# Inverse row sums of the attention spread over the partitions by way of DRAM instead of by transpositions, from the fifth pair on

## The chip, the cores and the metric

The kernel runs on one core of a Trainium2 chip. The metric is the device time of one execution in microseconds, as the median of the runs: 739.43 us (739.4 to 740.52, three runs). Engines: TensorE (PE; its weight loads are PEld), VectorE (DVE), ScalarE (ACT), GpSimd (POOL) and SyncE (SP), which here only issues DMAs.

## The reference

It is block-causal attention over 8 batches, 8 heads, 576 positions and a head size of 64, and then a gated MLP whose gate mixes positions. Cut to what matters:

```python
scores = scale * np.matmul(q, k.transpose(0, 1, 3, 2))
scores = np.where(mask, scores, -1000000000.0)
scores = scores - np.max(scores, axis=-1, keepdims=True)
attn = np.exp(scores)
attn = attn / (np.sum(attn, axis=-1, keepdims=True) + 1e-09)
x = np.matmul(attn, v)
h = gelu(x @ w_in); u, v = h[..., :512], h[..., 512:]
v_n = layer_norm(v) * g_ln
v_s = np.einsum('ts,bsd->btd', w_sg, v_n) + b_sg[None, :, None]
return x + (u * v_s) @ w_out
```

The change concerns the division by the row sums.

## The kernel before

**The work.** Attention is done by pairs of heads: 32 pairs, four (Q = 4) to a batch. The 576 rows of a pair are five row tiles (NT = 5), the first of 64 rows and four of 128. `Scores` makes the scores of a row tile on PE (tiles named s); DVE masks them and finds the negative maximum (negm), ACT takes the exponential and adds up each row on the way, into `sums`, a tile of 128 x 5 x 2: partition is the row within its tile, the columns are row tile and head.

**The values.** `Values` turns the exponentials on PE (banks pA, pB, pC for the full blocks, pd for the diagonal ones) and multiplies them with v (bank ob). The result lies transposed: partitions are the 2 x 64 columns of the two heads, the free axis is the 576 rows. So the inverse row sums, which lie one row to a partition, are needed along the free axis and in all 64 partitions of a head. `inverse` (L489) adds 1e-9, takes the reciprocal (r, 128 x 10), and has ACT spread r into rx (128 x 5 x 128, each number 64 times). `turn_sums` (L500) then does ten transpositions on PE, five of the diagonal blocks into pd and five of rx into the rest of pd and into pe, and two ACT copies take both banks to the tile rb. `normalise` (L536) multiplies on DVE with rb into x, and stores x to DRAM (spill). The 64 columns of the first row tile come from a free corner of pe (`self.o0`).

**The order.** One slot of the loop (L977) does pair n: it turns the exponentials of pair n (`turn("A0")` to `"C"`), then `turn_sums`, the first scores of pair n + 1, the products of pair n, `normalise`, the second scores of pair n + 1, and at the end `inverse` and `split_qk` for the pairs ahead. Between these, `hole(k)` places k units of the MLP of the batch before: a v part of 5 units, u, s and o parts of 8 units each, 29 over four slots. In the fourth slot of a batch come the spatial products (s part), in the third the out products (o part, bank acco), which add rows of spill (xr), and so on. In the first four slots (`opening_slot`) and the next four (`middle_slot`, with a list of steps written out by hand, `SCRIPT`) all engines keep the order of the code; these slots also load, split and transform the weights. From the ninth slot on (`slot`) only PE keeps it, and the scheduler orders the other engines' work (L978, L979).

**The queue of SP.** SP issues the DMAs, in each slot: six loads of v (`load_v`), one each of q and k for the pair after next (`load_qk`), the store of x, and loads of xr and stores of the output. In the first slots `fetch` adds weights: its list holds 16 parts of w_in, g_ln (g_bc), five steps of spatial weights (the last with b_sg) and 8 parts of w_out. `middle_slot` of pair 4 begins

```python
if n == Q:
    fetch(5)
load_v(n + 1)
load_qk(n + 2)
```

and its script fetches spatial weights, which POOL splits into ws_h and ws_l before it splits q and k (qh, ql, kh, kl) for pair 6.

Of the kernel before, what the change touches and what calls it, by code (L numbers as in the profile page):

```python
# [9 lines left out]
F32 = mybir.dt.float32  # L10
# [4 lines left out]
ALU = mybir.AluOpType  # L15
# [5 lines left out]
def kernel(  # L21
# [13 lines left out]
    B, H, D, S = qT.shape  # L35
    P = 128
    BLK = 64
# [4 lines left out]
    NT = (S + P - 1) // P  # L42
# [19 lines left out]
    vector = Engine("V", nc.vector)  # L62
# [3 lines left out]
    sync = Engine("S", nc.sync)  # L66

    cp = ctx.enter_context(tc.tile_pool(name="cp", bufs=1))
    sp = ctx.enter_context(tc.tile_pool(name="sp", bufs=1))
    dp = ctx.enter_context(tc.tile_pool(name="dp", bufs=2, space=DRAM))  # L70
# [6 lines left out]
    def page(dtype, n, name):  # L77
        tag, bufs = KINDS.get(name, KINDS["w"])
        return sp.tile([P, n], dtype, tag=tag, name=name, bufs=bufs)

    def bank(name):
        return psum.tile([P, 512], F32, tag="bank", name=name, bufs=8)
# [7 lines left out]
    def turn(out, in_):  # L90
        return tensor.transpose(out, in_, ident)

    def copy(e, dst, src):
        f = {"v": vector.tensor_copy, "a": scalar.copy, "g": gpsimd.tensor_copy}[e]
        return f(dst, src)
# [12 lines left out]
    def load_qk(n):  # L108
        b, h = PAIRS[n]
        q_f = sp.tile([P, S], F32, tag="q_f", name="q_f", bufs=1)  # L110
        k_f = sp.tile([P, S], F32, tag="k_f", name="k_f", bufs=1)
        q = qT[b, h : h + 2].rearrange("a d s -> (a d) s")
        k = kT[b, h : h + 2].rearrange("a d s -> (a d) s")
        if n == 0:
            for c in Q_PARTS:
                sync.dma_start(q_f[:, c], q[:, c])
            for c in K_PARTS:
                scalar.dma_start(k_f[:, c], k[:, c])
        else:
            sync.dma_start(q_f, q)  # L120
            behind["S"] = sync.dma_start(k_f, k)
        raw[n] = (q_f, k_f)

    def split_qk(n):
        out = []
        for x, t in zip(raw.pop(n), "qk"):
            hi = sp.tile([P, S], F32R, tag=t + "h", name=t + "h", bufs=1)
            lo = sp.tile([P, S], F32R, tag=t + "l", name=t + "l", bufs=1)
            if n:
                copy("g", hi, x)  # L130
                behind["G"] = gpsimd.tensor_tensor(lo, x, hi.bitcast(F32), op=ALU.subtract)
            out += [hi, lo]
        qk[n] = out
# [18 lines left out]
    def load_v(n, heads=(0, 1)):  # L152
        b, h = PAIRS[n]
        v_f, v_d = vals[n] = v_bufs[n % 2]
        lo, hi = slice(0, BLK), slice(BLK, P)
        for a in heads:
            r = (lo, hi)[a]
            cols = slice((h + a) * D, (h + a + 1) * D)
            x = v[b, : (NT - 1) * P, cols].rearrange("(j p) d -> p j d", p=P)
            if a == 0:  # L160
                sync.dma_start(v_f[:, :, r], x)
            else:
                sync.dma_start(v_f[lo, :, r], x[hi])
                sync.dma_start(v_f[hi, :, r], x[lo])
            sync.dma_start(v_d[r, : NT - 1, r], x[lo])
            sync.dma_start(v_d[r, NT - 1, r], v[b, S - TAIL :, cols])
# [24 lines left out]
    for s in (0, 1):  # L191
        t = cp.tile([P, NT - 1, 2 * D], F32, name=f"v_f{s}")
        d = cp.tile([P, NT, 2 * D], F32, name=f"v_d{s}")
        for a in (0, 1):
            r = slice(a * D, (a + 1) * D)
# [23 lines left out]
    W = 256  # L219
# [3 lines left out]
    def fetch(k=1):  # L223

        for _ in range(k):
            coming.popleft()()
# [118 lines left out]
    def weight_half():  # L345

        while weights:
            said = next(weights[0][1], None)
            if said is not None:
                return said  # L350
            weights.popleft()
# [106 lines left out]
    Q = H // 2  # L458
# [9 lines left out]
    class Values:  # L468
# [19 lines left out]

        def inverse(self):  # L489

            r = sp.tile([P, NT * 2], F32, tag="ri", name="r", bufs=2)
            vector.tensor_scalar_add(r, self.sm.rearrange("p i a -> p (i a)"), 1e-9)
            vector.reciprocal(r, r)
            self.rx = sp.tile([P, NT, 2 * D], F32, tag="rx", name="rx", bufs=1)
            scalar.copy(
                self.rx.rearrange("p i (a d) -> p (i a) d", a=2),
                r.unsqueeze(2).broadcast_to([P, NT * 2, D]),
            )

        def turn_sums(self):  # L500

            t, t2 = bank("pd"), bank("pe")
            W = NT * BLK
            for i in range(NT):
                c = slice(i * BLK, i * BLK + P)
                first = turned[:, BLK:] if i else ident
                tensor.transpose(t[:, c], pairs[i][:, P * i : P * (i + 1)], first)
            for i in (0, 1):
                turn(t[:, W + i * BLK : W + i * BLK + P], self.rx[:, i, :])
            for i in (2, 3, 4):  # L510
                turn(t2[:, P * (i - 2) : P * (i - 1)], self.rx[:, i, :])
            d = sp.tile([P, W + S], F32, tag="rb", name="rb", bufs=1)
            copy("a", d[:, :512], t)
            copy("a", d[:, 512:], t2[:, : 3 * P])
            self.dg = [d[:, i * BLK : (i + 1) * BLK] for i in range(NT)]
            self.rb = d[:, W:]
            self.o0 = t2[:, 3 * P : 3 * P + BLK]

        def products(self):
# [16 lines left out]
        def normalise(self):  # L536

            x = self.x = page(F32, S, "x")
            vector.tensor_tensor(x[:, BLK:], self.ob, self.rb[:, BLK:], op=ALU.mult)
            vector.tensor_tensor(x[:, :BLK], self.o0, self.rb[:, :BLK], op=ALU.mult)  # L540
            spill[self.b, self.p] = dp.tile([P, S], F32, tag="spill", name="spill", bufs=12)
            sync.dma_start(spill[self.b, self.p], x)

# [21 lines left out]
    def run_gelu():  # L565

        if side and side[0][0] == "G":
            side.popleft()[1]()
# [182 lines left out]
    def hole(k=1):  # L751

        while k > 0 and work:
            try:
                next(work[0])
                k -= 1
            except StopIteration:
                work.popleft()
# [15 lines left out]
    def split_pending():  # L774

        for f in pending:
            f()
        pending.clear()

    def opening_slot(n, va):  # L780

        va.turn("A0")
        va.turn("A1")
        va.turn("B0")
        va.turn("B1")
        va.inverse()
        split_pending()
        va.turn("C")
        load_qk(n + 2)
        load_v(n + 1)  # L790
        fetch(2 if n < Q - 1 else 4)
        nx = Scores(n + 1)
        for p in nx.FIRST:
            nx.products(*p)
        va.turn_sums()
        weight_half()
        for p in nx.FIRST:
            nx.softmax(*p)
        if n < Q - 1:
            nx.second()  # L800
            weight_half()
            split_qk(n + 2)
            weight_half()
            va.products()
            va.normalise()
            pending.append(va.split)
        else:
            weight_half()
            weight_half()
            va.products()  # L810
            va.normalise()
            va.split()
            nx.second()
        nv = Values(n + 1, nx)
        if n == Q - 1:
            nv.inverse()
            split_qk(n + 2)
            weight_half()
        return nx, nv
# [102 lines left out]
    def middle_slot(n, va):  # L922

        script = SCRIPT[n]
        g = [int(x) for x in FIRST[n % Q]]
        if n == Q:
            fetch(5)
        load_v(n + 1)
        load_qk(n + 2)
        va.turn("A0")  # L930
        va.turn("A1")
        if n != 2 * Q - 2:
            split_pending()
        run_gelu()
        hole(g[0])
        script[0]()
        va.turn("B0")
        va.turn("B1")
        hole(g[1])
        script[1]()  # L940
        va.turn("C")
        va.turn_sums()
        hole(g[2])
        script[2]()
        nx = Scores(n + 1)
        nx.first()
        va.products()
        va.normalise()
        nx.second()
        if n % Q == Q - 1:  # L950
            va.split()
        else:
            pending.append(va.split)
        script[3]()
        nv = Values(n + 1, nx)
        nv.inverse()
        split_qk(n + 2)
        script[4]()
        hole(g[3])
        script[5]()  # L960
        return nx, nv
# [70 lines left out]
```

## Time and profile before

| | |
|---|---|
| median of three runs | 739.43 us |
| the profiled execution's own time | 739.77 us |
| its span | 738.0 us |
| granted TensorE clock | 1.00 |
| pairs | 32 |
| DMA packets | 84731, 70.04 MB |

The span runs from the first to the last instruction of the profiled execution. Rows of a timeline or a chain give the start in us, the length in us, the engine, and what was written from what (the program's names) with a count; a bracket tells how long the engine had stood idle before it and what released it. Nearly all instructions are recorded by one helper (L60), so tiles tell them apart, not lines. PE's matmuls overlap: their lengths are longer than their distance, so the chain of waits gives the time that a group of them takes. SPq rows are DMAs issued by SP.

### The profile page before, as it was taken

What the parts mean: (1) busy time and instruction counts of PE and PEld (TensorE: products, weight loads), DVE (VectorE), ACT (ScalarE), POOL (GpSimd) and SP (SyncE); (2) the same over time, 40 slices, a digit from 0 to 9 for tenths busy, and PEclk for the clock granted to TensorE, in tenths of its full rate; (3) what the DMA queues carried; (4) which work ended last, traced back from release to release, by engine and by line L of the source; (5) the groups of instructions that cost most, each with busy time, mean ns of one, the idle gap of its engine ahead of it and who ended that gap; (6) DMA issues with size and microseconds to landing.
All of it is one profiled execution on the core that took longest, in us unless ns stands there. A gap on an engine that the chain in (4) does not pass through costs nothing.

```text
span 738.0 us, 18412 instructions
## 1 busy us (share of the span) xinstructions
PE 730.3 (99%) x6936; PEld 687.4 (93%) x6936; DVE 466.2 (63%) x1461; ACT 431.6 (58%) x1077; POOL 296.0 (40%) x361
## 2 busy tenths in 40 slices
PE   8999999999999999999999999999999999999997
PEld 7888999899998999989999899998999999998997
DVE  6998987579764396544956449554694456841732
ACT  7987888387544874458734577347783376712500
POOL 5767945455451244512345322453233533321120
PEclk9999999999999999999999999999999999999999
DMA  6667333143531225212342122422224221220032
GB/s 166 168 175 232 104 99 112 49 128 120 149 93 40 59 84 181 73 39 67 90 151 73 44 82 71 151 73 66 78 71 133 71 72 42 81 82 0 17 114 96
DMA packets 84731, 70.04 MB, mean 95 GB/s; under 512 B 59938, under 2 KB 60578, under 8 KB 84644
## 3 DMA queue, kind: packets, MB, share of 16 engines
q1 hardware_dynamic: 84356, 68.58, 31.7%
q8 instruction: 55, 0.90, 0.6%
q14 instruction: 32, 0.26, 0.1%
q10 hardware_dynamic: 288, 0.30, 0.1%
HBM read 49.98 MB, written 18.87 MB: 93 GB/s over the span
## 4 chain that ended last, share of the span: by engine, by line
PE 89%; DVE 6%; ACT 2%; issue 1%; DMA 1%; POOL 0%; SPq 0%; ACTq 0%; DVEq 0%
PE accs L60 16%; PE accv L60 14%; PE acco L60 13%; PE accu L60 12%; PE s L60 10%; PE ob L60 10%; PE pA L60 3%; PE pB L60 3%; PE pd L60 3%; ACT prob L60 2%; PE pC L60 2%; PE pe L60 2%; DVE prob L60 2%; DVE vl L60 1%; DMA q_f<-in_qT 0%
## 5 line engine op out<-in xcount | busy, mean ns | idle before, releaser
L60 ACT ACTIVATE prob<-prob,negm 128x576 f32<-128x576 f32 (+3 forms) x320 | 176.5, 554 | 54.7 <-DVE negm L60 53.2
L60 DVE CUSTOM_DVE_ANT_0 prob<-s,mask 128x256 f32<-128x256 f32 (+3 forms) x320 | 119.1, 417 | 40.7 <-PE s L60 39.2
L60 POOL TENSOR_TENSOR xh<-x,xh 128x64 fp32r<-128x64 f32 x32 | 10.8, 336 | 196.5 <-DVE xh L60 166.3
L60 POOL TENSOR_TENSOR gl<-u,gh 128x288 fp32r<-128x288 f32 x64 | 51.9, 814 | 89.0 <-DVE gh L60 73.6
L60 PE MATMUL accu<-xh,wi_h 128*128 128x288 f32 x256 | 78.3, 306 | 0.0
L60 PE MATMUL acco<-gh,wo_h 128*128 128x288 f32 x256 | 77.5, 303 | 0.4 <-DVE negm L60 0.2
L60 PE MATMUL accs<-ws_h,vh 128*128 128x288 f32 x256 | 77.9, 304 | 0.0
L60 PE MATMUL accu<-xl,wi_h 128*128 128x288 f32 x256 | 75.5, 295 | 0.0
L60 PE MATMUL accs<-ws_h,vl 128*128 128x288 f32 x256 | 75.5, 295 | 0.0
L60 PE MATMUL acco<-gh,wo_l 128*128 128x288 f32 x256 | 75.4, 295 | 0.0
L60 PE MATMUL accs<-ws_l,vh 128*128 128x288 f32 x256 | 75.4, 295 | 0.0
L60 PE MATMUL acco<-gl,wo_h 128*128 128x288 f32 x256 | 75.4, 295 | 0.0
L60 PE MATMUL accu<-xh,wi_l 128*128 128x288 f32 x256 | 75.4, 294 | 0.0
L60 DVE TENSOR_TENSOR u<-accs,u 128x288 f32<-128x288 f32 x64 | 29.2, 456 | 58.3 <-PE accs L60 53.6
L60 PE MATMUL accv<-wi_h,xh 128*128 128x512 f32 x160 | 65.3, 408 | 0.0
L60 PE MATMUL s<-kh,qh 64*128 64x320 f32 (+4 forms) x384 | 63.4, 322 | 0.5 <-DVE negm L60 0.5
L60 PE MATMUL accv<-wi_l,xh 128*128 128x512 f32 x160 | 62.8, 393 | 0.0
L60 ACT ACTIVATION_READ_ACCUMULATOR prob<-prob,negm 128x1 f32 x320 | 60.1, 188 | 0.0
L60 PE MATMUL s<-kh,ql 64*128 64x320 f32 (+4 forms) x384 | 59.0, 300 | 0.0
L60 PE MATMUL s<-kl,qh 64*128 64x320 f32 (+4 forms) x384 | 58.0, 299 | 0.0
L60 ACT COPY vv<-accv 128x512 f32<-128x512 f32 x32 | 18.6, 582 | 64.5 <-PE accv L60 64.5
L60 POOL CAST kh<-k_f 128x576 fp32r<-128x576 f32 x31 | 20.7, 667 | 75.7 <-PE s L60 75.7
(119 smaller groups left out, 2093.7 us busy)
## 6 DMA issues: line engine op xcount, KB each, us to landing
spill<-x SPq DMA_DIRECT2D x32, 288.0 KB, 2.7
xr<-spill SPq DMA_DIRECT2D x32, 288.0 KB, 3.1
out_T<-xr SPq DMA_DIRECT2D x32, 288.0 KB, 3.4
q_f<-in_qT SPq DMA_DIRECT2D x31, 288.0 KB, 3.1
k_f<-in_kT SPq DMA_DIRECT2D x31, 288.0 KB, 3.5
v_f<-in_v SPq DMA_DIRECT2D x32, 128.0 KB, 2.8
v_d<-in_v SPq DMA_DIRECT2D x64, 64.0 KB, 2.7
v_f<-in_v SPq DMA_DIRECT2D x64, 64.0 KB, 2.6
```

Source lines behind the costliest of these rows:

```text
L60: return lambda *a, **k: pin(method(*a, **k), self.letter)
```

## The change

For pairs 4 and up `inverse` calls the new `spread`: r is laid out by heads, stored to a DRAM tile of 2 x 640 numbers (a row for each head), and two DMAs read each row back into the 64 partitions of its head, into a part of the tile rb. `turn_sums` for these pairs does only the five transpositions of the diagonal blocks and copies 320 columns; rx, its five transpositions, bank pe and the second copy are not made. `self.o0` moves to a free corner of pd. The five fetches at the start of slot 4 move to the end of slot 3, ahead of the first `spread`.

```diff
         def inverse(self):
 
+            if self.n >= Q:
+                return self.spread()
...
+        def spread(self):
+
+            r = sp.tile([P, 2 * NT], F32, tag="ri", name="r", bufs=2)
+            vector.tensor_scalar_add(
+                r.rearrange("p (a i) -> p a i", a=2), self.sm.rearrange("p i a -> p a i"), 1e-9
+            )
+            vector.reciprocal(r, r)
+            rows = dp.tile([2, NT * P], F32, tag="rows", name="rows", bufs=2)
+            sync.dma_start(rows.rearrange("a (i p) -> p (a i)", p=P), r)
+            self.d = sp.tile([P, NT * (BLK + P)], F32, tag="rb", name="rb", bufs=1)
+            rb = self.d[:, NT * BLK :]
+            for a in (0, 1):
+                sync.dma_start(
+                    rb[a * D : (a + 1) * D, :], rows[a : a + 1, :].broadcast_to([D, NT * P])
+                )
+            self.rb = rb[:, BLK:]
+            self.r0 = rb[:, :BLK]
+
         def turn_sums(self):
 
-            t, t2 = bank("pd"), bank("pe")
+            t = bank("pd")
             W = NT * BLK
             for i in range(NT):
                 c = slice(i * BLK, i * BLK + P)
                 first = turned[:, BLK:] if i else ident
                 tensor.transpose(t[:, c], pairs[i][:, P * i : P * (i + 1)], first)
+            if self.n >= Q:
+                d = self.d
+                copy("a", d[:, :W], t[:, :W])
+                self.dg = [d[:, i * BLK : (i + 1) * BLK] for i in range(NT)]
+                self.o0 = t[:, 512 - BLK :]
+                return
+            t2 = bank("pe")
...
-            vector.tensor_tensor(x[:, :BLK], self.o0, self.rb[:, :BLK], op=ALU.mult)
+            vector.tensor_tensor(x[:, :BLK], self.o0, self.r0, op=ALU.mult)
...
         if n == Q - 1:
+            fetch(5)
             nv.inverse()
...
-        if n == Q:
-            fetch(5)
         load_v(n + 1)
         load_qk(n + 2)
```

More of the change, by code (lines that the diff above doesn't have):

```diff
@@ L511, in turn_sums @@
                 turn(t2[:, P * (i - 2) : P * (i - 1)], self.rx[:, i, :])
-            d = sp.tile([P, W + S], F32, tag="rb", name="rb", bufs=1)
+            d = sp.tile([P, NT * (BLK + P)], F32, tag="rb", name="rb", bufs=1)
             copy("a", d[:, :512], t)
-            copy("a", d[:, 512:], t2[:, : 3 * P])
+            copy("a", d[:, 512 : W + S], t2[:, : 3 * P])
             self.dg = [d[:, i * BLK : (i + 1) * BLK] for i in range(NT)]
-            self.rb = d[:, W:]
+            self.rb = d[:, W : W + S]
+            self.r0 = self.rb[:, :BLK]
             self.o0 = t2[:, 3 * P : 3 * P + BLK]
```

## The prediction

> **What bounds the kernel now.** I read the page first: its busy times and the chain that ended last.
>
> ```profile
> span 738.0 us, 18412 instructions
> PE 730.3 (99%) x6936; PEld 687.4 (93%) x6936; DVE 466.2 (63%) x1461; ACT 431.6 (58%) x1077; POOL 296.0 (40%) x361
> PE 89%; DVE 6%; ACT 2%; issue 1%; DMA 1%; POOL 0%; SPq 0%; ACTq 0%; DVEq 0%
> ```
>
> A busy PE alone proves little, since ends of matmuls are modelled; but the chain agrees: 89% of the time that set the end is PE's, 6% DVE's. Next the busy times by stretches, for four slots and then for one with the out part (columns: stretch, its length, busy us of PE, PEld, DVE, ACT, POOL).
>
> ```profile
> 296.00:390.00 94.00, 94.00 (x922) 89.19 (x922) 56.11 (x188) 53.70 (x135) 33.21 (x40) 1.00 0.29 83
> 346.00:368.00 22.00, 22.00 (x228) 21.52 (x224) 19.50 (x51) 16.52 (x37) 8.06 (x9) 1.00 0.34 98
> ```
>
> PE has no hole in 94 us, at a granted clock of 1.00: work taken from its queue shortens these slots one for one, until another engine stands in the way. DVE is the candidate: 60% over four slots, but 19.5 of 22 us in the slot with the out part. Last the chain of waits inside that slot, around the step that changes (start, length, what):
>
> ```profile
> 361.15 0.44 PE pC L60 x4
> 361.58 0.77 PE pd L60 x7
> 362.35 0.33 PE pe L60 x3
> 362.68 1.60 PE acco L60 x12
> ```
>
> Ten transpositions, seven into pd and three into pe, take 0.77 + 0.33 = 1.10 us, 0.11 each, and PE goes straight on with out products.
>
> **The change, part by part.** *Removed from PE:* five of those ten, 0.55 us per pair, for pairs 4 to 31: 28 x 0.55 = 15.4 us at most. The products still wait for ACT's copy of the diagonal blocks, as now. That copy and the reads write two parts of one tile; it waits for no read if hazards go by region, as they do for wi_l, whose u columns POOL writes while PE reads its v columns:
>
> ```profile
> 60.16 1.29 POOL L60 TENSOR_TENSOR wi_l<-w,wi_h 128x512 fp32r<-128x512 f32 x1
> ```
>
> ```profile
> 60.78 0.39 PE L60 MATMUL accv<-wi_l,xh 128*128 128x512 f32 x1
> ```
>
> *Removed from ACT:* the spreading copy of 0.72 us and the 0.49 us copy of pe; the copy of pd shrinks from 512 to 320 columns.
>
> ```profile
> L60 ACT COPY rx<-r 128x640 f32<-128x640 f32 x32 | 23.1, 723 | 16.6 <-DVE r L60 16.6
> L60 ACT COPY rb<-pe 128x384 f32<-128x384 f32 x32 | 15.6, 486 | 0.0
> ```
>
> That is over 1.2 us of ACT per slot. ACT is 2% of the chain, so I count it at nothing. The freed bank (pe) lets PE run a little further ahead of its readers: also nothing, but only ever a gain. DVE's addition and reciprocal on 128x10 keep their size.
>
> *Added: one DMA that writes 10 x 128 single words to DRAM, and two reads of 2,560 bytes into 64 partitions each.* The trace has no four-byte data write, so I bound it (packets, MB, share of 16 engines; then KB and median us to landing). The first row is queue q1 between 70.5 and 75.4 us, nearly all packets of 256 bytes; the rest is the whole run.
>
> ```profile
> q1 hardware_dynamic: 1780, 0.43, 39.0%
> ```
>
> ```profile
> q1 hardware_dynamic: 84356, 68.58, 31.7%
> ...
> k_f<-in_kT SPq DMA_DIRECT2D x31, 288.0 KB, 3.5
> v_f<-in_v SPq DMA_DIRECT2D x32, 128.0 KB, 2.8
> ...
> g_bc<-in_g_ln SPq DMA_DIRECT2D x1, 256.0 KB, 6.0
> ...
> v_d<-in_v SPq DMA_DIRECT2D x64, 16.0 KB, 2.2
> ```
>
> 0.39 x 16 x 4.9 us / 1780 = 17 ns of one DMA engine per packet of 256 bytes; over the whole run 0.317 x 16 x 738 / 84356 = 44 ns. The write's 1280 packets over 16 engines thus take 1.4 us at 17 ns, 3.5 us at 44. With the 2.2 us of the 16 KB load (64 packets) for the rest, the write lands after about 3.6 us, at most 5.7; I take 3.6, since a packet's own cost is nearer to the small packets' row. It could be below: 512 packets of v_f land after 2.8. The two reads together move 320 KB, so I take the 3.5 us of k_f. From r to rb: 3.6 + 0.7 (two issues) + 3.5 = 7.8 us.
>
> The Trainium skill ("DMA: Bandwidth & Descriptors", "Anatomy of one DMA") fits 2.0 us plus bytes over 436 GB/s to DMAs issued from GpSimd: 2.0 us for this write, and the sum below would end up to 3 us lower; the v_f row, 0.5 us over that fit's 2.3, speaks for counting packets.
>
> *Is it hidden?* In a steady slot, on DVE:
>
> ```profile
> 373.54 0.22 DVE L60 RECIPROCAL r<-r 128x10 f32<-128x10 f32 x1
> 391.77 0.69 DVE L60 TENSOR_TENSOR x<-ob,rb 128x512 f32<-128x512 f32 x1 [1.04 <-PE pe L60]
> ```
>
> r is ready at 373.8 and the product that needs rb starts at 391.8: 18 us for 7.8. What hides it is the slot's whole PE work. The new waits sit on SP, which stands still in a semaphore's wait (whole run: us, times, longest):
>
> ```profile
> SPq L60 <- POOL kl L60: 29.0, 13, 3.8
> ```
>
> Behind SP's wait for the write's landing are queued the next v, q and k loads, xr loads and out stores. In this slot k was issued at 378.5 and its cast on POOL began at 394.8, so 3.6 us of standing still do no harm:
>
> ```profile
> 378.46 0.38 SPq L60 DMA_DIRECT2D k_f<-in_kT  x1
> ```
>
> ```profile
> 394.84 0.66 POOL L60 CAST kh<-k_f 128x576 fp32r<-128x576 f32 x1
> ```
>
> *Slots 4 to 6 are another matter.* There SP, POOL, DVE and ACT keep the order of the code and POOL and DVE are full. The five fetches that move ahead of the inverse keep their place on SP, since nothing stood between; but slot 4's loads now come behind the write and reads for pair 4. SP, slot 4 (v_f is the first of v's six loads, xr are spatial weights):
>
> ```profile
> 57.64 0.33 SPq L60 DMA_DIRECT2D g_bc<-in_g_ln  x1
> 58.34 0.38 SPq L60 DMA_DIRECT2D v_f<-in_v  x1
> ...
> 64.64 0.90 SPq L60 DMA_DIRECT2D xr<-in_w_sgT  x2
> ```
>
> ```profile
> v_f<-in_v SPq DMA_DIRECT2D x1, 128.0 KB, 5.8
> ```
>
> g_bc landed 6.0 us after its issue, at 63.6, and this v_f, behind it, needed 5.8 us instead of 2.8: DMAs queue. The write for pair 4 (r ready at 55.4) takes v_f's place behind g_bc and lands at about 63.6 + 1.4 = 65.0; the reads are issued by 65.7, and v_f follows then, 7.4 us late. SP's 6.3 us from v_f to xr held some idle time, which a late start takes up; I take xr as 6.2 us late. On DVE:
>
> ```profile
> 55.21 0.22 DVE L60 RECIPROCAL r<-r 128x10 f32<-128x10 f32 x1
> ...
> 67.73 0.69 DVE L60 TENSOR_TENSOR x<-ob,rb 128x512 f32<-128x512 f32 x1 [0.20 <-PE pe L60]
> ...
> 97.63 0.48 DVE L60 TENSOR_SCALAR vone<-vv,rs 64x512 fp32r<-64x512 f32 x1
> ```
>
> x of pair 4, due at 67.7 less 0.55, waits until the reads land, 65.7 + 3.5 = 69.2; the softmax behind it loses 2 us, which DVE's idle time before slot 5 mostly takes. POOL is worse off:
>
> ```profile
> 68.97 0.67 POOL L60 CAST ws_h<-xr 128x576 fp32r<-128x576 f32 x1 [1.83 <-DMA xr<-in_w_sgT]
> ...
> 76.08 1.42 POOL L60 TENSOR_TENSOR kl<-k_f,kh 128x576 fp32r<-128x576 f32 x1
> ...
> 92.45 1.20 POOL L60 TENSOR_TENSOR rs<-rs,half 128x5 f32<-128x5 f32 x1
> ```
>
> It already waited for xr; now 6.2 us longer, so kl of pair 6 ends at 83.7 instead of 77.5. Its scores started on PE at 81.8 (80.7 with two slots' savings) and the third product of each part needs kl: PE stalls some 3 us in slot 5. POOL has hardly a pause up to rs, which ends at about 99.6 instead of 93.7; DVE's vone, then the norm's scales and the next softmax, start 2.0 us later than before, and PE already waits for that DVE chain at the end of slot 6:
>
> ```profile
> 81.84 1.58 PE s L60 x24
> ```
>
> ```profile
> 103.69 0.38 PE L60 MATMUL s<-kh,qh 64*128 64x320 f32 x1 [0.24 <-DVE negm L60]
> ```
>
> So I put the end of slot 6 at 2.0 us later than before, not 3 x 0.55 earlier. Per us by which the write is longer, this grows by up to 2 us, since the second pair of spatial weights stands behind the write for pair 5 too.
>
> *The out slots.* The first, slot 10, ends with PE waiting for DVE:
>
> ```profile
> 189.88 0.37 PE L60 MATMUL acco<-gh,wo_h 128*128 128x288 f32 x1 [0.24 <-DVE negm L60]
> ```
>
> There DVE keeps the 0.55; in the five later out slots it may keep some. I take 1.1 us off, between 0 and 6 x 0.55 = 3.3.
>
> **Sum:** 25 slots (7 to 31) x 0.55 = 13.75, less 2.0, less 1.1: 10.65 us. The profiled execution took 739.77 us (span 738.0), 0.34 above the median of 739.43; both lose the same, so the median becomes **728.8 us**.
>
> **The rivals.** *All of the gain comes* (0.16): the loads behind the write are not late enough to matter, or the extra bank covers it. For it: PE did not stall in slots 4 and 5 before; against it: SP's order is fixed there, and POOL waited for these weights even so. 739.4 - 15.4 = 724.0 to 726.
>
> *The small packets are dear* (0.16): 44 ns instead of 17 make the write 2.1 us longer, slots 4 to 6 lose 2 + 2 x 2.1 = 6.2 and the median is 739.4 - (13.75 - 1.1 - 6.2) = 733.0; at 60 ns, 3.4 us longer, 735.6.
>
> *The write is so slow that the kernel loses* (0.08). The gain of 12.65 outside slots 4 to 6 is gone when 2 + 2 x extra = 12.65, at a write 5.3 us longer, 8.9 us in all: 84 ns per packet. At 10 us it is 742. From 391.2 - 373.8 - 4.2 = 13.2 us on, the x of every slot waits as well. Against it: five times the row of the small packets; for it: no row shows writes this small. The Trainium skill ("DMA: Bandwidth & Descriptors", "Rules for kernel authors") speaks against this change: a strided last dimension becomes one descriptor per element, and a plain DMA with a rearranged pattern is no way to transpose, by its figure 19 times slower than the hardware's. No run here shows that ratio.
>
> *PE's savings become waits for DVE* (0.05): all out slots keep theirs and slots 4 to 6 cost 8: 13.75 - 3.3 - 8 = 2.5, 737. For it, DVE's 19.5 of 22; against it, 60% over four slots. That the change does less than it says isn't likely: PE's queue keeps the code's order, so the five are gone.
>
> **How the numbers follow.** The forecast has 0.55, with 726 to 731.5 for its own range. The range of 8 in 10 runs from 724.2 to 735.5: it leaves out the slowest write, the DVE case and the ends. A measurement of this kernel tells about 0.2%, 1.5 us, from no change. Faster by more (under 737.9) is the forecast, the full gain, the dear packets but for their tail, and half of the DVE case: 0.88; within, 0.04; slower, the slow write: 0.08.
>
> **What would show it.** Right: five pd transpositions and no pe in slots from 4 on; steady slots shorter by 0.55 us; the write landing after 3 to 5 us; POOL's ws_h in slot 4 at about 75 us and PE waiting in slot 5 for kl. Wrong: x waiting for DMA rb in steady slots, a write landing after 9 us or more, or PE idle before s or acco in most slots.

## The result and the profile after

The changed kernel takes 769.57 us (median of 4 runs, 767.53 to 771.59), the kernel before beside it 739.9 (739.4 to 740.52): 29.7 us slower, a ratio of 1.040 with an interval of 1.0368 to 1.0433. Nothing of the 10.65 us came, and the loss is nearly three times as large. First the page of the changed kernel, the lines that answer to those of before; its profiled execution took 768.53 us.

```profile
span 766.7 us, 18251 instructions
PE 726.9 (95%) x6796; PEld 680.3 (89%) x6796; DVE 467.8 (61%) x1461; ACT 397.2 (52%) x1021; POOL 302.6 (39%) x361
PE 59%; DVE 10%; DMA 6%; ACT 4%; issue 2%; POOL 2%; SPq 0%; DVEq 0%; ACTq 0%
```

PE has 140 matmuls fewer, five for each of 28 pairs, as forecast. But it is busy for 95% of the span instead of 99%, and of the chain that ended last only 59% is PE's. DMA, 1% before, has 6%, and DVE 10%. Slots in which nothing comes in the way, though, are what the prediction said. Here are stretches like the two of before (four slots, and a slot with the out part, slot 18; columns as there, then granted clock, DMA share and GB/s), and the chain inside the second:

```profile
324.60:418.60 94.00, 93.45 (x908) 88.30 (x907) 57.48 (x187) 48.96 (x126) 33.85 (x40) 1.00 0.40 97
383.00:404.40 21.40, 21.40 (x219) 20.88 (x219) 18.64 (x54) 15.23 (x34) 8.75 (x10) 1.00 0.31 90
```

```profile
390.21 0.54 PE pd L60 x5
```

Five transpositions into pd take 0.54 us, pe is gone, and from its first transposition to the next slot's this slot has 21.39 us instead of 21.94. So the loss sits elsewhere. Where, is read from the first transposition of each slot (start, length, PE's matmuls into pA), for slots 7, 9 and 11, before:

```profile
105.98 1.03 PE L60 MATMUL pA<-ident,prob 128*128 128x128 f32 x8
...
152.16 1.03 PE L60 MATMUL pA<-ident,prob 128*128 128x128 f32 x8
...
196.32 0.92 PE L60 MATMUL pA<-ident,prob 128*128 128x128 f32 x7
```

and after:

```profile
122.37 0.60 PE L60 MATMUL pA<-ident,prob 128*128 128x128 f32 x4
...
169.04 1.03 PE L60 MATMUL pA<-ident,prob 128*128 128x128 f32 x8
...
228.09 1.03 PE L60 MATMUL pA<-ident,prob 128*128 128x128 f32 x8
```

Slots 4 to 6 end 16.4 us later; slots 7 and 8 take 0.5 more (46.67 for 46.18); slots 9 and 10 take 14.9 more (59.05 for 44.16); from slot 11 to the end it is 3.0 less (538.6 for 541.7) where 11 were forecast (21 x 0.55, less what was left of the 1.1 after slot 10). The sum is 28.8, the difference of the spans but for rounding. The 8 us that are missing from slot 11 on lie in single slots, above all 19, 26 and 30; DVE's x waits there eight times for the reads, 1.7 to 4.9 us each, a sign that the prediction had named. How these waits reach PE was not followed.

The new DMAs (KB each, median us from issue to landing), and what SP and DVE waited for (us in all, times, longest):

```profile
rb<-rows SPq DMA_DIRECT2D x56, 160.0 KB, 3.5
...
rows<-r SPq DMA_DIRECT2D x28, 5.0 KB, 10.2
```

```profile
SPq L60 <- DMA rows<-r: 260.9, 28, 10.7
```

```profile
DVE x L60 <- DMA rb<-rows: 38.6, 11, 5.2
```

The reads land after the 3.5 us that were taken for them. The write of 1280 single words lands after 10.2 us, not 3.6 and not 5.7, and SP stands still 261 us for it. In slot 4 SP issues (start, length) and POOL waits for the spatial weights so:

```profile
55.47 0.80 SPq L60 DMA_DIRECT2D rows<-r  x1
65.89 1.11 SPq L60 DMA_DIRECT2D rb<-rows  x2
...
73.22 0.90 SPq L60 DMA_DIRECT2D xr<-in_w_sgT  x2
```

```profile
78.51 0.67 POOL L60 CAST ws_h<-xr 128x576 fp32r<-128x576 f32 x1 [12.94 <-DMA xr<-in_w_sgT]
```

The weights' loads leave 8.6 us later than before (64.64) and their cast starts 9.5 us later (68.97). PE then waits for kh and kl in slot 5, 5.6 us, and in slot 6 it waits 6.4 us for ACT's exponentials, which themselves stand 11.0 us until POOL has filled a part of `sums`. In slot 9 the chain that ended last runs from DMA to DMA (start, length):

```profile
151.86 9.71 DMA rows<-r
...
172.81 12.91 DMA xr<-in_w_out
```

The last of these is an ordinary load, of 256 KB, which took 3.5 us before. It was issued half a microsecond behind a write of single words and needed 12.9 us. The forecast held no such term: it let SP wait for the write, but did not let a load behind the write be late by itself.

### The profile page after: what moved, and what is told of

Same layout as the page of the kernel before. It is cut to its first block, busy times and chain, and to the rows that moved or that the text cites. A ratio compares the mean times of both kernels' runs of the same rounds, so it can differ in the third digit from the quotient of the medians.

```text
span 766.7 us, 18251 instructions
## 1 busy us (share of the span) xinstructions
PE 726.9 (95%) x6796; PEld 680.3 (89%) x6796; DVE 467.8 (61%) x1461; ACT 397.2 (52%) x1021; POOL 302.6 (39%) x361
## 4 chain that ended last, share of the span: by engine, by line
PE 59%; DVE 10%; DMA 6%; ACT 4%; issue 2%; POOL 2%; SPq 0%; DVEq 0%; ACTq 0%
PE accs L60 14%; PE acco L60 10%; PE accv L60 10%; PE accu L60 7%; PE ob L60 6%; PE s L60 5%; DMA rows<-r 3%; ACT prob L60 2%; POOL rs L60 2%; PE pB L60 2%; PE pA L60 2%; DVE prob L60 2%; DMA xr<-in_w_out 2%; PE pd L60 2%; DVE bs L649 2%
## 5 line engine op out<-in xcount | busy, mean ns | idle before, releaser
L60 PE MATMUL s<-kh,qh 64*128 64x320 f32 (+4 forms) x384 | 65.9, 326 | 7.4 <-POOL kh L60 4.9
L60 DVE TENSOR_TENSOR x<-ob,rb 128x512 f32<-128x512 f32 x32 | 22.0, 689 | 58.6 <-DMA rb<-rows 38.6
L60 PEld LDWEIGHTS s<-kh,qh 64*128 64x128 f32 x384 | 38.9, 188 | 18.7 <-issue 7.9
```

What stands on the lines that cost most here:

```text
L60: return lambda *a, **k: pin(method(*a, **k), self.letter)
```

## The experiments

The question is what of the write costs: its number of packets, its single words, or SP's standing still for it; and whether the rest of the prediction holds once the write is cheap. The kernel before took 739.77 us on the chip of m1, e1, e2 and e4, 739.46 on that of e5 to e8, 739.66 on that of e3, e10 and e11.

**A price list, m1_prices.** It computes nothing of the reference: it runs the change's DMAs and variants of them, four times each, in a single run.

```diff
+nc.sync.dma_start(near.rearrange("a (i p) -> p (a i)", p=P), r)
...
+nc.sync.dma_start(half.rearrange("a (i p) -> p (a i)", p=P), r[:, :5])
...
+nc.sync.dma_start(far.rearrange("(c p) n -> p c n", p=P)[:, :, 0], r)
...
+nc.sync.dma_start(gap.rearrange("p (c t) -> p c t", t=2)[:, :, 0], r)
...
+nc.sync.dma_start(twos.rearrange("(c p) t -> p c t", p=P), r.rearrange("p (c t) -> p c t", t=2))
...
+nc.sync.dma_start(flat, r)
...
+nc.sync.dma_start(inside.rearrange("p (c t) -> p c t", t=2)[:, :, 0], r)
...
+nc.sync.dma_start(big.rearrange("(c p) n -> p c n", p=P), wide.rearrange("p (c n) -> p c n", n=64))
...
+nc.sync.dma_start(back, near.rearrange("a (i p) -> p (a i)", p=P))
```

> This kernel computes nothing of the reference: it fills the output with ones and then issues DMAs one at a time, each waiting for the landing of the one before, four times round: 1280 single words to DRAM in the change's pattern (near), half as many (half), 1280 words 512 bytes apart (far), 1280 words with each partition's ten beside each other with gaps (gap), 640 pairs of words (twos), 128 runs of 40 bytes (flat), 1280 words into SBUF (inside), 1280 runs of 256 bytes to DRAM (big), ten rows of 512 bytes (tenrow), 1280 single words read from DRAM (back), and the two broadcast reads (rb). Theory A, the price hangs on the number of packets whatever their target: near, far, gap, inside and back all land after 8 to 10 us, half after about 6, flat under 3. Theory B, words written to DRAM that lie beside each other get in each other's way: near 8 to 10 us, far 3 to 4, inside 3 to 4, back 3 to 4. Theory C, any short write to DRAM is slow to land: near, far, gap 8 to 10 us, inside and back 3 to 4, big 3 to 5.

The DMA issues of this kernel (KB each, median us to landing):

```profile
rb<-near SPq DMA_DIRECT2D x8, 160.0 KB, 12.0
big<-wide SPq DMA_DIRECT2D x4, 320.0 KB, 3.3
near<-r SPq DMA_DIRECT2D x4, 5.0 KB, 11.6
back<-near SPq DMA_DIRECT2D x4, 5.0 KB, 2.4
half<-r SPq DMA_DIRECT2D x4, 2.5 KB, 9.7
...
gap<-r SPq DMA_DIRECT2D x4, 5.0 KB, 8.8
twos<-r SPq DMA_DIRECT2D x4, 5.0 KB, 4.0
flat<-r SPq DMA_DIRECT2D x4, 5.0 KB, 1.4
```

Packets don't set the price: 640 packets of one word (half) need 9.7 us, 640 packets of two words (twos) 4.0, and 1280 packets of 256 bytes (big, 64 times the bytes) 3.3. Reading 1280 single words (back) needs 2.4. Not every DMA ran alone: half ran beside rb's reads, and near stood first behind the output's writes and then beside big. But the first near has no packet in any engine from 28.0 us on and lands at 36.5, so it is not another DMA's packets that it waits for; and gap and twos ran alone. For the words into SBUF (inside) and those 512 bytes apart (far) no landing is recorded, but the next DMA, which waits for it, bounds it. Behind far it is issued after 5.4 us at most, behind inside after 2.9. So single words written to DRAM are dear, in these three patterns the more the closer they lie, and short writes as such are not. That is nearest to theory B, which had no price for gap. And rb's reads, which take 3.5 us in the kernel, took 12.0 beside the words of half.

**The change with a cheap write, e1_flat_write.**

```diff
-rows = dp.tile([2, NT * P], F32, tag="rows", name="rows", bufs=2)
-sync.dma_start(rows.rearrange("a (i p) -> p (a i)", p=P), r)
+rows = dp.tile([P, 2 * NT], F32, tag="rows", name="rows", bufs=2)
+sync.dma_start(rows, r)
+rows = rows.rearrange("(a x) c -> a (x c)", a=2)
```

> The write goes out as 128 runs of 40 bytes instead of 1280 single words; the reads take the same number of bytes, but the numbers come back in the wrong order (the output is not the reference's). All else is the change. My theory, that the landing time of the write is the whole of the loss: the write lands after 2.5 to 3 us, slots 4 to 6 and 9 take what they took before or less, and the median is 725 to 730 us. Rival, that the loss comes from the added waits on SP and from the reads, whatever the write costs: still 755 us or more. Second rival, that another order of the engines' queues in the later slots costs something of its own: 732 to 745.

731.99 us (730.77 to 732.09), ratio 0.9892 (0.9876 to 0.9909): inside the range of the first prediction (724.2 to 735.5), though not in that of this run's own theory, with nothing changed but the shape of the write (and the order of the numbers). It lands after 1.7 us. PE's first transpositions of slots 7, 9 and 11:

```profile
111.79 1.03 PE L60 MATMUL pA<-ident,prob 128*128 128x128 f32 x8
...
199.81 0.93 PE L60 MATMUL pA<-ident,prob 128*128 128x128 f32 x7
```

Slots 7 to 10 are 2.3 us shorter than before, and from slot 11 to the end (span 730.3) it is 11.2 for 21 slots, 0.53 each; so the later slots lose nothing, though the time is the foot of the second rival's. But slots 4 to 6 end 5.8 us later, not 2.0. PE, in slot 5 (the brackets: idle time before and what ended it), and then its windows (busy us, granted clock, DMA share, GB/s):

```profile
83.00 0.39 PE L60 MATMUL s<-kh,qh 64*128 64x256 f32 x2 [2.73 <-POOL kh L60]
84.47 0.58 PE L60 MATMUL s<-kl,qh 64*128 64x256 f32 x2 [0.97 <-POOL kl L60]
```

```profile
80.00:84.00 4.00, 0.77 (x6) 1.00 0.42 86
84.00:88.00 4.00, 3.53 (x30) 0.50 0.76 251
88.00:92.00 4.00, 4.00 (x57) 0.65 0.09 33
```

PE stands 3.7 us, near the 3 of the prediction, but longer for kh than for kl. Then, busy again, it is granted 0.50 of its clock for 3.5 us and 0.65 for 4 more: another 3.5 x 0.50 + 4 x 0.35 = 3.2 us. 3.7 + 3.2 less the slot's 0.55 is 6.35, and slot 5 is 6.4 us longer (22.04 for 15.63). The end of slot 6 is set elsewhere. There PE waits for DVE's negm again, 1.2 us instead of 0.5, and the chain that ended last leads from that wait back over DVE and ACT to POOL, not over PE (the first row is PE's, at the end of slot 6):

```profile
108.89 0.38 PE L60 MATMUL s<-kh,qh 64*128 64x320 f32 x1 [0.94 <-DVE negm L60]
```

```profile
94.09 0.35 ACT L60 ACTIVATE prob<-prob,negm 64x64 f32<-64x64 f32 x1 [5.61 <-POOL sums L60]
```

```profile
92.58 1.43 POOL L60 TENSOR_TENSOR ws_l<-xr,ws_h 128x576 fp32r<-128x576 f32 x1
93.95 0.10 POOL L60 MEMSET sums<- 128x2 f32 x1
```

`Scores` has POOL fill a part of `sums`, into which ACT adds the rows. In slot 5 this stands on POOL behind the second pair of spatial weights, so ACT's exponentials wait 5.6 us for it; before, ACT had no such wait, and in the changed kernel it waits 11.0 us there. ACT's sums then hold up DVE, whose vone comes at 103.06 us instead of 97.63: 5.4 later, where 2.0 was forecast. The prediction had counted PE's wait and POOL's rs, but neither the clock nor this wait of ACT. No run moved the filling of `sums`, so what it costs by itself is not measured.

**The reads a slot later, e2_late_reads.** The write stays as in the change; the reads go to the next slot, behind that slot's loads of v, q and k, so that these do not stand behind SP's wait.

```diff
+            self.rows = rows
+
+        def reads(self):
+
+            rows = self.rows
...
+        if n >= Q:
+            va.reads()
         va.turn("C")
```

> The write is as in the change; the two reads are issued in the next slot, behind its loads of v, q and k and its first fetches, so that SP has nothing of that slot left to hold back when it waits for the write. If what costs is SP standing still with the loads queued behind it, most of the loss in slots 4 to 6 goes and the median is 735 to 745 us. If the loads, though issued, stand behind the write in the DMA queues themselves until it has landed, the loss stays: 755 to 770.

789.57 us (784.11 to 795.55), ratio 1.0678 (1.0618 to 1.0738): worse than the change. DVE waited for the reads 74.9 us in 15 waits instead of 38.6 in 11. Taking SP's wait away from these loads didn't help; but since x waits longer, this run alone doesn't say whether SP's standing or something else makes the loads late.

**The same price again, with nobody waiting for it.** Three kernels carry e1's cheap write and the change's reads. Behind the reads they also issue the 1280 single words once more, to a tile that nobody reads: e5 on SP's queue into DRAM, e6 on ACT's queue into DRAM, e11 on SP's queue into SBUF.

```diff
 # e5_dummy_sync
+slow = dp.tile([2, NT * P], F32, tag="slow", name="slow", bufs=2)
+sync.dma_start(slow.rearrange("a (i p) -> p (a i)", p=P), r)
 # e6_dummy_act
+scalar.dma_start(slow.rearrange("a (i p) -> p (a i)", p=P), r)
 # e11_words_inside
+slow = sp.tile([P, 4 * NT], F32, tag="rx", name="slow", bufs=1)
+sync.dma_start(slow.rearrange("p (c t) -> p c t", t=2)[:, :, 0], r)
```

> The write as in e1 (128 runs of 40 bytes, so the order of the numbers is wrong), the reads as in the change, and behind the reads, on the same queue, the change's single-word write once more, into a second DRAM tile that nobody reads. Nobody waits for that write; only the v, q, k and weight loads of the next slot stand behind it in SP's DMA queue. Theory D, what costs is that SP stands still 10 us until the words have landed and so issues the loads late: SP does not stand here, 732 us as with the cheap write alone (up to 734). Theory Q, what costs is that every DMA behind the words in the same queue is late, whoever waits: the loads land up to 10 us late as in the changed kernel, slots 5, 6 and 9 lengthen as there, 750 to 770.

772.07 us (771.64 to 773.83), ratio 1.0445 (1.043 to 1.0461): the whole loss of the change is back, though nothing is computed from these words. On SP, the start of slot 5, and the chain that ended last:

```profile
82.67 0.59 SPq L60 DMA_DIRECT2D slow<-r  x1
83.30 0.71 SPq L60 DMA_DIRECT2D v_f<-in_v  x1
```

```profile
83.30 10.78 DMA v_f<-in_v
```

SP issued v_f right behind the words, without waiting for them, and v_f, 2.8 us before, needed 10.78. Four times, 16.1 us in all, SP did wait for these words to land, and 64.0 us for the cheap write, where the change has 28 waits of 260.9 us. So taking SP's standing still away saves nothing: loads that are issued at once, behind the words, come late all the same.

> As e5, but the extra single-word write that nobody waits for is issued from ScalarE's queue (order of the numbers wrong as in e1). ACT pays for one DMA issue per slot, about 0.4 us, and a wait for r. Theories D and Q both give 732 to 738, since SP's queue holds no words. Theory M, the words hold up every DMA of the core whatever its queue (at the DMA engines or at the memory): 745 to 770, with late loads as in e5 under Q.

761.46 us (759.72 to 763.91), ratio 1.030 (1.0278 to 1.0321). Another queue takes off only a quarter of the loss: 29 us above e1 for 40. ACT issued the words, SP the 128 cheap runs just behind them; the busy tenths of the DMA engines from 55 to 80 us, 0.625 us each, stand last, with ACT's queue in this stretch (packets, MB, share of 16 engines):

```profile
56.54 0.39 ACTq L60 DMA_DIRECT2D slow<-r  x1
```

```profile
57.17 0.33 SPq L60 DMA_DIRECT2D rows<-r  x1
66.56 1.11 SPq L60 DMA_DIRECT2D rb<-rows  x2
```

```profile
DMA  9999999943000000000037637414445799988996
...
q10 hardware_dynamic: 2523, 0.01, 6.3%
```

The cheap write, which let the reads go after 4.8 us in e1 (issued at 56.76, reads at 61.55), needed 9.4 here; and from 61.3 us on, for the last five of these microseconds, the engines' busy share is a nought. The packets have gone; what is awaited is their landing. The words' packets were cheap: 0.063 x 16 x 25 us / 2523 = 10 ns of an engine each. In all, SP waited 162.7 us for the cheap write.

> e5 with one thing changed: the 1280 single words that nobody waits for go into an SBUF tile (each partition's ten words 8 bytes apart) instead of DRAM, same queue, same place, same number of packets; the order of the numbers is wrong as in e1. Theory M, writing single words to DRAM holds up the memory: 731 to 734, as the cheap write alone. Rival, 1280 packets of any kind in the queue hold up what stands behind them: 755 to 772, as e5.

733.6 us (733.3 to 733.93), ratio 0.9914 (0.9899 to 0.9928). As many packets, of as many bytes, at the same place of the same queue cost 1.6 us more than e1 where they go to SBUF, and 40 where they go to DRAM. Their landing here (the cheap write lands after 1.8 us):

```profile
slow<-r SPq DMA_DIRECT2D x28, 5.0 KB, 2.5
```

So it is the writing of single words to DRAM that holds up other DMAs too, in its own queue (e5) and in another (e6).

**The forecast's own price, e7_twos.**

```diff
-rows = dp.tile([2, NT * P], F32, tag="rows", name="rows", bufs=2)
-sync.dma_start(rows.rearrange("a (i p) -> p (a i)", p=P), r)
+rows = dp.tile([NT * P, 2], F32, tag="rows", name="rows", bufs=2)
+sync.dma_start(
+    rows.rearrange("(c p) t -> p c t", p=P), r.rearrange("p (c t) -> p c t", t=2)
+)
+rows = rows.rearrange("(a x) t -> a (x t)", a=2)
```

> The change with the same bytes written as 640 packets of 8 bytes (order of the numbers wrong), which alone landed after 4.0 us: nearly the price of 3.6 us that the prediction put in. If the price of the write was all that the prediction got wrong, its own sum gives 728.8 + 2 x 0.4 = 729.6. With the end of slot 6 at 5.8 us later, as the cheap write in e1 had it, and the prediction's 2 us per us of longer write, 732 + 2 x 2.6 = 737; with no such growth 732.

737.14 us (734.68 to 737.32), ratio 0.996 (0.9946 to 0.9974), with the write landing after 4.3 us:

```profile
rows<-r SPq DMA_DIRECT2D x28, 5.0 KB, 4.3
```

So near the 3.6 us that the prediction took, the forecast of 728.8 would have been 8 us too low, and the measured time outside its range (up to 735.5): the price was not all that it had wrong. The 737 of the growing loss is met, but partly by chance: slot 7 starts at 115.58 us in this execution, 3.8 later than in e1, and 1.2 of that was there before slot 1. The write's 2.6 us more than in e1 (4.3 for 1.7) cost 2.6 in slots 4 to 6, about 1 us per us, where up to 2 were forecast.

**From the ninth pair on, e3_from_ninth.** The change with `self.n >= 2 * Q` in place of `self.n >= Q`, and the five fetches back at their old place.

> The change, but only from the ninth pair on; pairs 0 to 7 as before, fetches of slot 4 at their old place; the whole reference is computed. If the loss has separate places (slots 4 to 6, then slots 9 and 10, then some slots later), slots 4 to 6 are as before and the rest loses what it lost in the changed kernel: 739.4 - 24 x 0.55 + 15 (slots 9 and 10) + 8 (later slots) = about 749. If slots 9 and 10 lose only because slots 4 to 6 came late: about 735.

759.35 us (758.14 to 760.81), ratio 1.0261 (1.024 to 1.0283). PE's first transpositions of slots 9 and 11:

```profile
151.60 1.04 PE L60 MATMUL pA<-ident,prob 128*128 128x128 f32 x8
...
206.53 0.93 PE L60 MATMUL pA<-ident,prob 128*128 128x128 f32 x7
```

Slot 9 starts 0.56 us earlier than before, as it should, and slots 9 and 10 still take 54.9 us for 44.2. So their loss is their own and doesn't follow from slots 4 to 6. From slot 11 to the end (span 757.8) it is 9.6 us longer than before, where the changed kernel was 3.0 shorter; here the expectation was too low. What a write costs in a later slot may depend on which loads are issued close behind it; this was not tried.

**One transposition instead of five.** r itself is turned on PE, 128x10 to 10x128, so that DRAM gets ten rows of 512 bytes; the reads are the change's.

```diff
...
+t = bank("pe")
+turn(t[: 2 * NT, :P], self.r)
+rt = sp.tile([2 * NT, P], F32, tag="rx", name="rt", bufs=1)
+copy("a", rt, t[: 2 * NT, :P])
 rows = dp.tile([2, NT * P], F32, tag="rows", name="rows", bufs=2)
-sync.dma_start(rows.rearrange("a (i p) -> p (a i)", p=P), r)
+sync.dma_start(rows.rearrange("a (i p) -> (a i) p", p=P), rt)
```

In e4 this stands behind turn B1 of every slot from the fifth on; in e8 it is moved behind the second script step of slots 4 to 7; in e10 only pairs from the ninth on have it, as in e3.

> The whole of the reference is computed. r (128 x 10) is turned on PE by one transposition right after turn B1 of the next slot, ACT copies 10 x 128 to SBUF, and ten rows of 512 bytes go to DRAM; the reads are the change's. It takes four of ten transpositions from PE instead of five: 28 x 0.44 = 12.3 us. My theory (the price of the single-word write is the loss): the write lands after 2 to 2.5 us, DVE waits for rb in few slots, and the median is 727 to 733 us. Rival (a DRAM round trip in SP's order costs by itself): above 740.

732.9 us (731.78 to 733.76), ratio 0.9909 (0.9894 to 0.9924): faster than both kernels. Slot 5 still takes 18.4 us for 15.6. In slot 4 x had waited 3.87 us for the reads, and in slot 5 PE stood before the transposition of r:

```profile
78.69 0.28 PE L60 MATMUL pe<-ident,r 128*10 128x128 f32 x1 [1.72 <-DVE w L60]
```

r had been ready since 76.1 us; what released PE is DVE's work on w, a weight's part, which comes after r in DVE's order. For kh and kl PE did not wait in this run.

> e4 (one transposition of r on PE, ten rows to DRAM), with the transposition and its DMAs moved behind the second script step of slots 4 to 7, so that the spatial weights' fetch of slot 4 is issued ahead of the write and the reads; the whole reference is computed. If e4's 2.7 us in slot 5 came from that fetch standing behind the write: slot 5 back to 15.6 us and 730 us in all. If it came from the transposition waiting for DVE's reciprocal: 732.9 as e4.

734.36 us (734.07 to 736.58), ratio 0.9939 (0.9923 to 0.9956). Slot 5 is back to 17.3, but slot 4 grows from 22.4 to 26.9, by a wait that neither side of the expectation had:

```profile
73.08 0.69 DVE L60 TENSOR_TENSOR x<-ob,rb 128x512 f32<-128x512 f32 x1 [7.16 <-DMA rb<-rows]
```

So in e4 PE waited neither for the late weights nor for the reciprocal. With the round trip ahead of the weights' loads (e4) as behind them (e8), x of pair 4 waits for the reads, 3.87 and 7.16 us: slot 4 has no room for it.

> e4 (one transposition of r on PE, its ten rows of 512 bytes to DRAM, the change's reads), but only from the ninth pair on; pairs 0 to 7 as before; the whole reference is computed. Slots 4 to 7 as before, slots 8 to 31 shorter by 0.44 us each: 739.4 - 10.6 = 728.8. If e4's late loads of the last feed-forward come again, 1 to 2 us more, 730.5. If nothing in slots 4 to 6 had cost e4 anything, it is no better than e4: 732.9 or more.

730.83 us (730.0 to 731.38), ratio 0.9875 (0.986 to 0.989): 8.8 us faster than before and the fastest kernel here. Its page, and a piece of its slot 20 on the chain that ended last:

```profile
PE 719.9 (99%) x6840; PEld 676.9 (93%) x6840; DVE 469.0 (64%) x1461; ACT 407.0 (56%) x1053; POOL 296.0 (41%) x361
```

```profile
399.18 0.11 PE pe L60
```

96 transpositions less at 0.11 us are 10.6, and PE is busy 10.4 less; one of 0.11 remains in pe. PE is full again, at 99% of a span of 728.2 us. Most of what is missing to 728.8 lies in slot 31 and the end, 0.6 us longer than before where 0.4 less was due.

## Why the prediction was wrong

**What bounds the kernel, and what a transposition is worth: right.** Five of them were worth 0.55 us per slot wherever nothing else came in the way (slot 18: 21.39 for 21.94), and with a cheap write that is nearly everywhere from slot 7 on.

**The write's price: the step that failed.** The prediction took 3.6 us by the time that packets of 256 bytes take in a DMA engine, and at most 5.7 by the mean of all packets. It measured 10.2. The packets were not the error: by e6's row a word takes 10 ns of an engine, less than the 17 that were taken. But such a row tells how long an engine is busy with a packet, and the words have left the engines long before they have landed. None of the rows quoted showed a write of single words, so they could not bound this one from above; the rival's 8.9 us was nearer to the truth than the upper end. The prediction had named a landing after 9 us or more as the sign that it is wrong, and it is the sign that came. By the Trainium skill's fit ("DMA: Bandwidth & Descriptors", "Anatomy of one DMA") an estimate for it is 2.0 us. That fit is of DMAs issued from GpSimd; for this write, issued from SP, the 10.2 us measured decide. The Trainium skill's rule against a strided last dimension ("DMA: Bandwidth & Descriptors", "Rules for kernel authors") had the right sign. One descriptor per element, which that rule of the Trainium skill names, is not enough as a cause here: as many one-word packets into SBUF land after 2.5 us.

**Only SP waits: wrong, and a term that was missing.** The prediction let the write hurt through SP's order alone. e5 shows the whole loss with 16 us of that wait in place of 261, e6 three quarters of it from another queue, e11 almost nothing (1.6 us) with the words in SBUF. A load behind the words is itself late: 10.78 us for v_f, 12.91 for xr in slot 9. The prediction's rival had no term for that, and so none for slots 9 and 10, where 14.9 us were lost. The measured time stands 27 us above the 742 that the rival gave for a write of 10 us: some 15 of them are slots 9 and 10, 8 are the slots from 11 on, and little is left for slots 4 to 6, where the rival's 2 + 2 x 6.4 = 14.8 stands beside 16.4 measured.

**Slots 4 to 6: mis-sized, with a wait left out.** With the cheap write the spatial weights' cast came at 74.74 us for 75 forecast, PE waited 3.7 us for kh and kl where 3 for kl were forecast, and POOL's rs ended at 100.6 for 99.6. Slot 6 ends, as forecast, on DVE's chain. Yet vone, on that chain, came 5.4 us later and not 2.0, and the slots ended 5.8 us later. The prediction counted ACT at nothing; but ACT's exponentials of slot 5 stood 5.6 us until POOL had filled `sums`, behind the late weights. It also left out that PE, once it has stood, gets 0.50 to 0.65 of its clock for some 7.5 us, which lengthens slot 5. With the slow write the slots ended 16.4 later. In e7, with a write of 4.3 us, the median of 737.14 us lies above the 735.5 that ended the range, and slots 4 to 6 are the main part of that.

**The out slots: too pessimistic.** 1.1 us was taken off for DVE; with the cheap write five of the six gave their 0.55 or more, and only slot 30 gave nothing.

**The reads and the copy: right.** The reads landed after 3.5 us; among what PE waited for in e1 there is no copy of pd. (`load_v` issues seven loads to a pair, not six; the prediction took their time from the rows, so no sum hangs on it.)

## What to carry to other kernels

A price that no row shows is not bounded by rows of another direction or packet size: a DMA that writes single words to DRAM deserves a run of its own, or a shape that avoids it (one transposition on PE before the write made 37 us of difference here, e4 against the change). Its cost is not the wait of its issuer alone: DMAs that were issued in the ten microseconds behind it came late too. A stall of PE costs its length and then, in the one place where both were read (slot 5 of e1: 3.7 and 3.2 us), nearly as much again in granted clock. And where all engines keep the order of the code, an engine that is off the critical path, as ACT was with 2% of the chain, comes onto it when what stands ahead of its small inputs is late.

## What the runs showed of the hardware

Single words into DRAM: 1280 of them, neighbours in DRAM coming from different partitions, land after 10.2 to 11.6 us; 8 bytes apart after 8.8; 512 bytes apart in 5.4 at most; the same 5 KB as 640 packets of 8 bytes in 4.0, as 128 runs of 40 bytes in 1.4; 1280 words into SBUF in 2.5. Meanwhile the DMA engines show next to no packets (e6, from 61.3 us on), and loads and writes of this queue and of another land 5 to 9 us late. So it is not the engines' time for the packets; whether the memory holds the words up, or the engines hold other DMAs back until the memory has answered, was not shown.

The granted clock falls where PE stands: in the changed kernel's slot 9 (columns: busy us, granted clock, DMA share, GB/s)

```profile
175.00:180.00 5.00, 0.73 (x6) 0.89 0.59 23
180.00:185.00 5.00, 0.00 (x0) 0.50 0.35 34
185.00:190.00 5.00, 2.74 (x13) 0.50 0.85 264
```

and it is 0.50 when PE starts again. Over the whole span it is 0.982 there, 0.999 in e10 and 1.0 in the kernel before.
